# A 3200-point filter by FFT, then a gated convolution: the transform factored as 100 by 32 instead of 128 by 25

## The chip, the cores and the metric

The kernel runs on one core of a Trainium2 chip. The core has a matrix engine (TensorE, PE in the profile; PEld is its loading of weights), a vector engine (VectorE, DVE), an activation engine (ScalarE, ACT), a general one (GpSimd, POOL) and SyncE (SP), which here only issues transfers; 16 DMA engines move the data. Each engine works through its own queue in order and waits on semaphores. Matmuls write to PSUM, and ACT or DVE must copy ("evict") the result to SBUF. The metric is device time in microseconds. The kernel before took 382.9 us (median of three runs, 381.12 to 385.6).

## What is computed

For each of 8 sequences of 3200 positions by 256 channels, a global filter in the frequency domain, and then a gated linear unit whose gate is a causal convolution of 5 taps.

```python
X = np.fft.rfft(x, axis=1)                       # x: 8 x 3200 x 256
x = np.fft.irfft(X * (filt_r + 1j*filt_i), n=3200, axis=1)
gate_pre = sum(conv_w[k] * xp[:, k:k+S, :] for k in range(5))   # xp: x with 4 zero rows ahead
out = (1/(1+np.exp(-gate_pre)) * (x @ w_val)) @ w_out
```

Inputs and output are float32.

## The kernel before, in words

The transform of 3200 is split as 128 by 25 (`L`, `R`). Everything is done per sequence ("batch") in chunks, and the tables of sines and cosines are made on the core in a set-up part (lines 91 to 284, mostly DVE, with ACT's Sin and POOL's iota).

- `load_x` (L86): POOL issues a transfer that also casts to bf16; seven chunks of 3 or 4 residues (`PCH`), 128 partitions each.
- `s1` (L307): a matmul with `cf_t` does the 128-point transform; DVE evicts to `so` (L310), SP writes it to a DRAM scratch `dscr` (L312).
- `load_t` (L326 to L329): after all seven chunks, SP reads `dscr` back in another order, so that the 25 residues of 5 frequencies lie on 125 partitions (`tt`). This trip through DRAM is the forward relayout.
- `s2` (L340 to L346): twiddle and 25-point transform as one real matrix per group of 5 frequencies; 13 groups, two to a chunk, four matmuls of 125x128 weights by 256 columns each. ACT evicts to `xs` (L349). DVE multiplies by the filter (`za` L354, `zb` L358) and adds (`z` L360).
- `inva` (L376, L378): the inverse of that, again four matmuls of 256 columns per group; ACT evicts to `u` (L381), SP writes a second scratch `escr` (L392).
- `load_v`, `invb` (L413): `escr` is read back as `vt`; one matmul of 128 columns per residue and channel half; ACT evicts to `yt` (L415) with the channels on the partitions. POOL copies a small halo (L420, L422).
- `conv` (L431): the five taps as 64x64 diagonal matmuls, 20 to a chunk; ACT evicts with Sigmoid to `gt` (L436). `val` (L448): four matmuls; DVE multiplies by the gate (`gv`, L453). `outp` (L465): two matmuls per residue; DVE or ACT by turns evict to `o` (L470, L473), SP stores it (L475).

All stages share one PSUM pool of four buffers of 128 x 1024 float32. The order of the work is a hand-written loop: at each step, a chunk of every stage, each with a fixed lag (`LAG_S2`, `LAG_IB`), so that several batches are under way at once; each evicting engine is fixed by the stage.

Of the kernel before, what the change touches and what calls it, by code (L numbers as in the profile page):

```python
# [15 lines left out]
PI = math.pi  # L16

L = 128
R = 25
NG = 13
GL = 5
NQ = 2 * NG
P2 = GL * R

PCH = [(0, 4), (4, 4), (8, 4), (12, 3), (15, 3), (18, 3), (21, 4)]
ICH = [PCH[-1]] + PCH[:-1]  # L30
GCH = [(0, 2), (2, 2), (4, 2), (6, 2), (8, 2), (10, 2), (12, 1)]
NCH = 7
# [3 lines left out]
def kernel(  # L36
# [9 lines left out]
):  # L46
    nc = tc.nc
    B, S, D = x.shape
    N = S
    K = moe_conv_w.shape[0]  # L50
    assert D == 256 and S == L * R and K == 5
    H = K - 1

    cpool = ctx.enter_context(tc.tile_pool(name="const", bufs=1))
    cf_t = cpool.tile([128, 130], FP16, name="cf_t")
    ci_t = cpool.tile([128, 128], FP16, name="ci_t")
    wc_t = cpool.tile([128, NG, 128], FP16, name="wc_t")
    ws_t = cpool.tile([128, NG, 128], FP16, name="ws_t")
    wsn_t = cpool.tile([128, NG, 128], FP16, name="wsn_t")
    vc_t = cpool.tile([128, NG, 128], FP16, name="vc_t")  # L60
    vs_t = cpool.tile([128, NG, 128], FP16, name="vs_t")
    vsn_t = cpool.tile([128, NG, 128], FP16, name="vsn_t")
    fr_t = cpool.tile([128, NG, D], BF16, name="fr_t")
    fm_t = cpool.tile([128, NG, 2, D], BF16, name="fm_t")
# [3 lines left out]
    b_npi = cpool.tile([128, 1], FP32, name="b_npi")  # L68
# [3 lines left out]
    xpool = ctx.enter_context(tc.tile_pool(name="xin", bufs=10))  # L72
    spool = ctx.enter_context(tc.tile_pool(name="s1o", bufs=4))
    tpool = ctx.enter_context(tc.tile_pool(name="s2i", bufs=8))
# [4 lines left out]

    xts = {}  # L80

    def load_x(b, j):
        p0, np_ = PCH[j]
        xt = xpool.tile([128, 4, D], BF16, name="xt")
        src = x[b].rearrange("(a r) d -> a r d", r=R)[:, p0:p0 + np_, :]
        nc.gpsimd.dma_start(out=xt[:, 0:np_, :], in_=src)  # L86
        xts[(b, j)] = xt

    for j in range(NCH):
        load_x(0, j)  # L90


    with tc.tile_pool(name="gen", bufs=1) as g1, \
         tc.tile_pool(name="gen2", bufs=2) as g2, \
         tc.tile_pool(name="genf", bufs=1) as gf:

        def floormod(src_ap, divisor):
            shp = list(src_ap.shape)
            divi = g2.tile(shp, I32, name=f"fm_i{shp[1]}")
            bak = g2.tile(shp, FP32, name=f"fm_b{shp[1]}")  # L100
            q = g2.tile(shp, FP32, name=f"fm_q{shp[1]}")
            cm = g2.tile(shp, FP32, name=f"fm_c{shp[1]}")
            nc.vector.tensor_scalar(divi[...], src_ap, 1.0 / float(divisor), None,
                                    op0=ALU.mult)
            nc.vector.tensor_copy(bak[...], divi[...])
            nc.vector.scalar_tensor_tensor(q[...], bak[...], -float(divisor), src_ap,
                                           op0=ALU.mult, op1=ALU.add)
            nc.vector.tensor_scalar(cm[...], q[...], float(divisor) - 0.5, None,
                                    op0=ALU.is_ge)
            nc.vector.scalar_tensor_tensor(q[...], cm[...], -float(divisor), q[...],  # L110
                                           op0=ALU.mult, op1=ALU.add)
            nc.vector.tensor_scalar(cm[...], q[...], -0.5, None, op0=ALU.is_lt)
            nc.vector.scalar_tensor_tensor(q[...], cm[...], float(divisor), q[...],
                                           op0=ALU.mult, op1=ALU.add)
            return q

        def iota(shape, pattern, base, cm, name):
            t = g1.tile(shape, FP32, name=name)
            nc.gpsimd.iota(t[...], pattern=pattern, base=base, channel_multiplier=cm,
                           allow_small_or_imprecise_dtypes=True)  # L120
            return t

        nc.vector.memset(b_npi[:, :], -PI)
        pcol = iota([128, 1], [[0, 1]], 0, 1, "pcol")


        kc = iota([128, NG, 2, GL], [[5, NG], [0, 2], [1, GL]], 1, 0, "kc")
        nc.vector.memset(kc[:, NG - 1, 0, GL - 1:GL], 0.0)
        pr = g1.tile([128, NG, 2, GL], FP32, name="pr")
        nc.vector.tensor_scalar(pr[...], kc[...], pcol[:, 0:1], None, op0=ALU.mult)  # L130
        nc.vector.tensor_scalar(pr[:, :, 0, :], pr[:, :, 0, :], 0.75 * L, None,
                                op0=ALU.add)
        q = floormod(pr[...].rearrange("p g c l -> p (g c l)"), L)
        nc.scalar.activation(cf_t[:, :], q[...], AF.Sin, bias=b_npi[:, 0:1],
                             scale=2.0 * PI / L)

        ident = g1.tile([128, 128], FP32, name="ident")
        nc.vector.memset(ident[:, :], 1.0)
# [3 lines left out]
        idh = g1.tile([128, 128], FP16, name="idh")  # L142
        nc.vector.tensor_copy(idh[:, :], ident[:, :])


        rq = floormod(pcol[...], R)
        lp = g1.tile([128, 1], FP32, name="lp")
        nc.vector.tensor_tensor(lp[...], pcol[...], rq[...], op=ALU.subtract)
        nc.vector.tensor_scalar(lp[...], lp[...], 1.0 / R, None, op0=ALU.mult)
        rp = g1.tile([128, 1], FP32, name="rp")  # L150
        nc.vector.tensor_copy(rp[...], rq[...])
        lw = g1.tile([128, 1], FP32, name="lw")
        nc.vector.tensor_scalar(lw[...], pcol[...], 4.0 * R - 0.5, None, op0=ALU.is_ge)
        nc.vector.tensor_scalar(lw[...], lw[...], -65.0, None, op0=ALU.mult)


        mk = g1.tile([128, GL, R], FP16, name="mk")
        mkf = g1.tile([128, GL, R], FP32, name="mkf")
        nc.vector.memset(mkf[...], 1.0)
        nc.gpsimd.affine_select(out=mkf[...], in_=mkf[...], pattern=[[-R, GL], [0, R]],  # L160
                                compare_op=ALU.is_ge, fill=0.0, base=0,
                                channel_multiplier=1)
        nc.gpsimd.affine_select(out=mkf[...], in_=mkf[...], pattern=[[R, GL], [0, R]],
                                compare_op=ALU.is_ge, fill=0.0, base=R - 1,
                                channel_multiplier=-1)
        nc.vector.tensor_copy(mk[...], mkf[...])

        def expand(dst, src):
            nc.gpsimd.memset(dst[:, :, P2:128], 0.0)
            for g in range(NG):  # L170
                nc.vector.tensor_tensor(
                    dst[:, g, 0:P2].rearrange("p (l r) -> p l r", l=GL),
                    src[:, g, :].unsqueeze(1).to_broadcast((128, GL, R)),
                    mk[...], op=ALU.mult)

        def negate(dst, src):
            nc.vector.tensor_scalar(dst[...], src[...], -1.0, None, op0=ALU.mult)

        def sincos(prod, dc, ds, dsn):
            qs = floormod(prod[...].rearrange("p g r -> p (g r)"), N)  # L180
            sn = g2.tile([128, NG, R], FP16, name="sn")
            nc.scalar.activation(sn[...].rearrange("p g r -> p (g r)"), qs[...],
                                 AF.Sin, bias=b_npi[:, 0:1], scale=2.0 * PI / N)
            pc = g2.tile([128, NG, R], FP32, name="pc")
            nc.vector.tensor_scalar(pc[...], prod[...], 0.75 * N, None, op0=ALU.add)
            qc = floormod(pc[...].rearrange("p g r -> p (g r)"), N)
            cs = g2.tile([128, NG, R], FP16, name="cs")
            nc.scalar.activation(cs[...].rearrange("p g r -> p (g r)"), qc[...],
                                 AF.Sin, bias=b_npi[:, 0:1], scale=2.0 * PI / N)
            expand(dc, cs)  # L190
            expand(dsn, sn)
            negate(ds, dsn)

        HK = R // 2 + 1
        kv = g1.tile([128, NG, R], FP32, name="kv")
        nc.gpsimd.iota(kv[:, :, 0:HK], pattern=[[5, NG], [L, HK]], base=1,
                       channel_multiplier=0, allow_small_or_imprecise_dtypes=True)
        nc.gpsimd.iota(kv[:, :, HK:R], pattern=[[5, NG], [-L, R - HK]],
                       base=1 + L * (R - 1), channel_multiplier=0,
# [352 lines left out]
```

## Time and profile before

| what | value |
|---|---|
| runs | 385.6, 381.12, 382.9 us; median 382.9 |
| profiled execution: its span, first to last instruction | 385.9 us (0.8% above the median of the runs) |
| granted clock, mean over the span | 0.966 |
| PE, DVE, ACT, POOL busy | 312.3, 284.9, 229.1, 64.2 us |
| DMA | 94.53 MB, mean 245 GB/s |
| first eviction of stage 2 (`xs`), first of the inverse (`yt`) | 47.1 us, 93.7 us |
| first `out` matmul of each batch | 116.1, 154.4, 193.2, 233.7, 273.6, 310.0, 342.6, 364.6 us |

The page gives no other time for the profiled execution than its span. The page counts an engine as busy from an instruction's start to its end. Matmuls are pipelined, so neighbours overlap and a PE that is always "busy" need not be streaming all the time. "Slices" are 40 equal parts of the span (9.65 us each), with the busy share in tenths. "Stretches" give for a window the busy time and number of instructions of each engine, then the granted clock, the DMA share and GB/s. The timeline lists start, duration, engine, line, operation, output from input, tile shape and count, and in brackets the idle time ahead and what ended it.

### The profile page before, as it was taken

What the parts mean: (1) busy time and instruction counts of PE and PEld (TensorE: products, weight loads), DVE (VectorE), ACT (ScalarE), POOL (GpSimd) and SP (SyncE); (2) the same over time, 40 slices, a digit from 0 to 9 for tenths busy, and PEclk for the clock granted to TensorE, in tenths of its full rate; (3) what the DMA queues carried; (4) which work ended last, traced back from release to release, by engine and by line L of the source; (5) the groups of instructions that cost most, each with busy time, mean ns of one, the idle gap of its engine ahead of it and who ended that gap; (6) DMA issues with size and microseconds to landing.
All of it is one profiled execution on the core that took longest, in us unless ns stands there. A gap on an engine that the chain in (4) does not pass through costs nothing.

```text
span 385.9 us, 8019 instructions
## 1 busy us (share of the span) xinstructions
PE 312.3 (81%) x3089; PEld 206.9 (54%) x3089; DVE 284.9 (74%) x462; ACT 229.1 (59%) x255; POOL 64.2 (17%) x131
## 2 busy tenths in 40 slices
PE   0230477475899999999997999899999999999992
PEld 0100145253656756766675666566676677666661
DVE  4999958553858887888787789678977677765554
ACT  1100235334976777677765776677677878867660
POOL 8797211112110211021102011100010001001000
PEclk9999998766989999999999999999999999999998
DMA  7999999999999999999999999989595968449343
GB/s 124 144 162 190 216 257 251 231 250 280 179 250 249 311 286 273 263 282 332 274 301 303 286 269 298 285 299 319 201 351 170 304 223 299 136 142 323 141 191 152
DMA packets 94118, 94.53 MB, mean 245 GB/s; under 512 B 10102, under 2 KB 74624, under 8 KB 94080
## 3 DMA queue, kind: packets, MB, share of 16 engines
q1 hardware_dynamic: 80064, 78.98, 62.5%
q0 software_dynamic: 14016, 15.04, 28.1%
q8 instruction: 24, 0.39, 0.4%
q14 instruction: 14, 0.11, 0.1%
HBM read 56.59 MB, written 52.43 MB: 282 GB/s over the span
## 4 chain that ended last, share of the span: by engine, by line
PE 44%; DVE 20%; DMA 19%; SPq 8%; issue 4%; ACT 2%; POOL 1%; DVEq 0%; ACTq 0%; POOLq 0%
PE ps L431 12%; PE ps L448 7%; DMA escr<-u 6%; PE ps L465 6%; DVE so L310 6%; DMA vt<-escr 5%; SPq L326 5%; PE ps L413 5%; DMA dscr<-so 4%; PE ps L376 3%; DVE gv L453 3%; DMA tt<-dscr 3%; PE ps L378 3%; PE ps L307 3%; DVE za L354 2%
## 5 line engine op out<-in xcount | busy, mean ns | idle before, releaser
L415 ACT ACTIVATE yt<-ps 128x1024 bf16<-128x1024 f32 (+1 forms) x56 | 52.1, 931 | 44.3 <-PE ps L413 44.2
L453 DVE TENSOR_TENSOR gv<-ps,gt 128x1024 bf16<-128x1024 f32 (+1 forms) x56 | 61.9, 1104 | 18.7 <-PE ps L448 13.7
L310 DVE CAST so<-ps 128x1024 bf16<-128x1024 f32 (+1 forms) x56 | 61.5, 1103 | 19.0 <-PE ps L307 15.9
L354 DVE TENSOR_TENSOR za<-xs,fr_t 125x1024 bf16<-125x1024 bf16 (+1 forms) x56 | 37.3, 665 | 50.5 <-ACT xs L349 50.3
L381 ACT ACTIVATE u<-ps 125x1024 bf16<-125x1024 f32 (+1 forms) x56 | 53.9, 963 | 24.4 <-PE ps L378 21.6
L431 PE MATMUL ps<-yt,dg_t 64*64 64x512 bf16 (+1 forms) x1120 | 65.7, 361 | 0.8
L349 ACT ACTIVATE xs<-ps 125x1024 bf16<-125x1024 f32 (+1 forms) x56 | 54.0, 965 | 19.6 <-PE ps L346 18.4
L436 ACT ACTIVATE gt<-ps 128x1024 bf16<-128x1024 f32 (+1 forms) x56 | 52.4, 935 | 9.1 <-PE ps L431 5.9
L86 POOL DMA_DIRECT2D xt<-in_x_dram x56 | 30.2, 569 | 153.0 <-PE ps L307 146.5
L307 PE MATMUL ps<-xt,cf_t 128*128 128x512 bf16 x112 | 36.9, 421 | 22.4 <-DVE so L310 11.4
L465 PE MATMUL ps<-wo_t,gv 128*128 128x256 bf16 x400 | 52.8, 273 | 0.9 <-DVE gv L453 0.9
L448 PE MATMUL ps<-yt,wv_t 128*128 128x512 bf16 (+1 forms) x224 | 52.6, 357 | 0.0
L465 PEld LDWEIGHTS <-gv 128*128 128x128 bf16 x400 | 39.1, 98 | 14.9 <-DVE gv L453 1.2
L413 PE MATMUL ps<-ci_t,vt 128*128 128x128 f16 x400 | 31.9, 221 | 13.3 <-DMA vt<-escr 9.6
L431 PEld LDWEIGHTS <-dg_t 64*64 64x64 bf16 x1120 | 30.1, 106 | 23.2 <-issue 10.1
L340 PE MATMUL ps<-tt,wc_t 125*128 125x256 bf16 x104 | 30.1, 289 | 12.9 <-DMA tt<-dscr 10.6
L470 DVE COPY o<-ps 128x1024 f32<-128x1024 f32 (+1 forms) x32 | 36.7, 1148 | 1.1 <-PE ps L465 1.1
L360 DVE TENSOR_TENSOR z<-za,zb 125x1024 bf16<-125x1024 bf16 (+1 forms) x56 | 36.4, 650 | 1.3
L413 PEld LDWEIGHTS <-vt 128*128 128x128 bf16 x400 | 27.0, 98 | 17.9 <-DMA vt<-escr 10.7
L358 DVE TENSOR_TENSOR zb<-xs,fm_t 125x1024 bf16<-125x1024 bf16 (+1 forms) x56 | 36.2, 646 | 0.0
L376 PE MATMUL ps<-z,vc_t 125*128 125x256 bf16 x104 | 30.0, 289 | 6.9 <-DVE z L360 6.9
L307 PEld LDWEIGHTS <-cf_t 128*128 128x128 f16 x112 | 9.2, 108 | 41.7 <-issue 28.2
(109 smaller groups left out, 386.6 us busy)
## 6 DMA issues: line engine op xcount, KB each, us to landing
out_dram<-o SPq DMA_DIRECT2D x32, 512.0 KB
tt<-dscr SPq DMA_DIRECT2D x48, 256.0 KB
escr<-u SPq DMA_DIRECT2D x48, 224.0 KB
out_dram<-o SPq DMA_DIRECT2D x24, 384.0 KB
xt<-in_x_dram POOLq DMA_DIRECT2D x32, 256.0 KB, 6.5
dscr<-so SPq DMA_DIRECT2D x32, 256.0 KB
vt<-escr SPq DMA_DIRECT2D x32, 256.0 KB
xt<-in_x_dram POOLq DMA_DIRECT2D x24, 192.0 KB, 5.7
```

The costliest lines, as they stand in the source:

```text
L307: nc.tensor.matmul(ps[:, a * D:e * D], lhsT=cf_t[:, 0:128], rhs=xt[:, a:e, :], start=True, stop=True)
L310: nc.vector.tensor_copy(so[:, 0:np_, :].rearrange("p a d -> p (a d)"), ps[:, 0:np_ * D])
L349: nc.scalar.activation(xs[0:P2, 0:ng, :, :].rearrange("p g c d -> p (g c d)"), ps[0:P2, 0:ng * 512], AF.Copy)
L354: nc.vector.tensor_tensor(za[0:P2, 0:ng], xs[0:P2, 0:ng], fr_t[0:P2, g0:g0 + ng, :].unsqueeze(2).to_broadcast((P2, ng, 2, D)), op=ALU.mult)
L381: nc.scalar.activation(u[0:P2, 0:2 * ng, :].rearrange("p q d -> p (q d)"), ps[0:P2, 0:ng * 512], AF.Copy)
L413: nc.tensor.matmul(ps[:, o:o + L], lhsT=v[:, a, 128 * dh:128 * dh + 128], rhs=ci_t[:, :], start=True, stop=True)
L415: nc.scalar.activation(y[:, :, H + p0:H + p0 + np_, :].rearrange("p h a n -> p h (a n)"), ps[:, :].rearrange("p (h n) -> p h n", h=2)[:, : ...
L431: nc.tensor.matmul(ps[64 * dh:64 * dh + 64, 512 * r:512 * r + np_ * L], lhsT=dg_t[rows, dh, k, :], rhs=y[rows, dh, p0 + k:p0 + k + np_, :] ...
L436: nc.scalar.activation(g[:, :, 0:np_ * L], ps[:, :].rearrange("p (h n) -> p h n", h=2)[:, :, 0:np_ * L], AF.Sigmoid)
L448: nc.tensor.matmul(ps[:, 512 * eh:512 * eh + np_ * L], lhsT=wv_t[:, dh, 128 * eh:128 * eh + 128], rhs=y[:, dh, H + p0:H + p0 + np_, :], st ...
L453: nc.vector.tensor_tensor(gv[:, :, 0:np_ * L], ps[:, :].rearrange("p (h n) -> p h n", h=2)[:, :, 0:np_ * L], g[:, :, 0:np_ * L], op=ALU.mult)
L465: nc.tensor.matmul(ps[:, D * a:D * a + D], lhsT=gv[:, eh, L * a:L * a + L], rhs=wo_t[:, eh, :], start=(eh == 0), stop=(eh == 1))
```

## The change

The transform is factored as 100 by 32. The real input makes 51 of the 100 first-stage frequencies enough, kept as two halves of 26 with real and imaginary part, each padded to 32 rows: four quarters of 32 partitions.

- Stage 1 takes the 256 channels as 128 pairs, and for all 32 residues of a batch evicts into one tile `so` (pair, residue, two channels; runs of 4 residues x 2 channels). It has one buffer.
- The forward relayout is four DVE instructions per batch (`turn`): transposes of 32x32 blocks of 4-byte words (a word is a pair of bf16), from `so` to `tt`, within each quarter. The scratch `dscr` and both its transfers are gone.
- Stage 2 is a 64x64 matmul per frequency of 256 columns, read from `tt` as pairs 128 bytes apart; real and imaginary parts are the two halves of the 64. Four such matmuls stand on the four quadrants of the array. Its inverse `inva` is two of them per frequency, on `za` (spectrum times filter's real part) and `zb` (times its imaginary part); they are summed in PSUM, so that the DVE addition `z` is gone.
- The inverse relayout still goes through the scratch `escr`, now in single writes of 128 partitions; its reads are split into 96 and 8 partitions, the output stores into 96 and 4. The x loads have 100 partitions and eight chunks.
- The order is no longer the loop with lags. A list scheduler (`Plan`) is given every task with an engine, a cost in us, a rank (its place in time, eight ranks to a batch), what it depends on and the buffers it takes and gives; it plays the tasks through and writes the queues of all engines in that order. Evictions `so`, `xs`, `u`, `o` go to ACT or DVE, whichever the plan finds free (as planned, ACT has 159 full and 8 half ones, DVE 65 and 8). The plan charges 0.1 us for a change between 64x64 and whole-array matmuls, and prefers to stay.
- The tables are made in fewer, larger DVE operations (`frac` in place of `floormod`), with three 128 x 1664 products on POOL.

```diff
-L = 128
-R = 25
+L = 100
+R = 32
...
     def s1(b, j):
+        xt = st.pop(("X", b, j))
+        xv = xt[0:L].rearrange("p r (q e) -> p q r e", e=2)
         ps = psum()
+        for h in range(2):
+            nc.tensor.matmul(ps[:, 512 * h:512 * h + 512],
+                             lhsT=cf_t[0:L].rearrange("p h c i -> p (h c i)"),
+                             rhs=xv[:, 64 * h:64 * h + 64], start=True, stop=True)
...
+    def so(b, j, e):
+        if ("SO", b) not in st:
+            st["SO", b] = sopool.tile([128, DP, R, 2], BF16, name="so")
+        ps = st.pop(("s1", b, j))
+        copy(e, st["SO", b][:, :, RC * j:RC * j + RC, :].rearrange("p q r e -> p q (r e)"),
+             ps[:, :].rearrange("p (q n) -> p q n", q=DP))
...
+        dst = st["T", b][:, w * q:w * q + w].rearrange("p q r e -> p (q r e)").bitcast(FP32)
+        nc.vector.transpose(dst, src)
...
     def s2(b, u):
+        for a in range(nm):
+            for h, t in ((0, 0), (1, 1), (0, 1), (1, 0)):
+                i = 2 * (m0 + a) + t
+                rows = slice(64 * h, 64 * h + 64)
+                nc.tensor.matmul(ps[64 * t:64 * t + 64, 512 * h + D * a:512 * h + D * a + D],
+                                 lhsT=w_t[rows, i, :], rhs=t_[rows, :, i, :],
+                                 start=True, stop=True)
...
     def inva(b, u):
+            for w, tab in enumerate((a_t, b_t)):
+                for t, h in ((0, 0), (1, 1), (0, 1), (1, 0)):
+                    rows = slice(64 * t, 64 * t + 64)
+                    nc.tensor.matmul(
+                        ps[64 * h:64 * h + 64, 512 * t + D * a:512 * t + D * a + D],
+                        lhsT=tab[rows, NM * h + m0 + a, :],
+                        rhs=zz[w][rows, h, D * a:D * a + D],
+                        start=(w == 0), stop=(w == 1))
...
+        nc.sync.dma_start(out=v[0:96], in_=sv[0:96])
+        nc.sync.dma_start(out=v[96:NV], in_=sv[96:NV])
...
+        nc.sync.dma_start(out=dst[0:96], in_=o[0:96])
+        nc.sync.dma_start(out=dst[96:L], in_=o[96:L])
...
+    plan = Plan(dict(ps=4, xt=NXT, so=1, t=2, xs=3, za=3, zb=3, u=4, e=2, v=NVB, y=2, g=NGB,
+                     gv=NGB, o=NOB))
...
+            add(f"s1{b},{j}", {"PE": 0.45}, t0 + j, dep, lambda e, b=b, j=j: s1(b, j),
+                take=("ps",) + (("so",) if j == 0 else ()), give=("xt",), mode=0)
+            add(f"so{b},{j}", two(0.97, 1.15), t0 + j, [f"s1{b},{j}"],
+                lambda e, b=b, j=j: so(b, j, e), give=("ps",))
...
+            add(f"t{b},{q}", {"DVE": 1.15}, t0 + NCH, [f"so{b},{j}" for j in range(NCH)]
+                + ([f"t{b},{q - 1}"] if q else []),
+                lambda e, b=b, q=q: turn(b, q), take=("t",) if q == 0 else (),
+                give=("so",) if q == 3 else ())
...
+            add(f"wr{b},{u}", {"SP": 0.45}, r + 1, [f"ue{b},{u}"] + ([f"wr{b},{u - 1}"] if u else []),
+                lambda e, b=b, u=u: wr(b, u), take=("e",) if u == 0 else (), land=3.0)
...
+            add(f"lv{b},{i}", {"SP": 0.8}, r - 2, [f"wd{b},{u}" for u in range(len(UCH))],
+                lambda e, b=b, i=i: lv(b, i), take=("v",), land=3.0,
+                give=())
```

More of the change, by code (lines that the diff above doesn't have):

```diff
@@ L16, with __init__, add, run @@
 PI = math.pi
-L = 128
-R = 25
[L24 to L32, printed above, removed]
+L = 100
+R = 32
+NS = 26
+NM = 13
+NV = 4 * NS
+RC = 4
+NCH = R // RC
+UCH = [(m, min(2, NM - m)) for m in range(0, NM, 2)]
+ICH = [NCH - 1] + list(range(NCH - 1))
+MAGIC = 12582912.0
+class Plan:
+    def __init__(self, room, stay=1.0):
+        self.tasks, self.room, self.stay = {}, dict(room), stay
+    def add(self, name, engines, rank, deps, emit, take=(), give=(), land=0.0, mode=None):
+        self.tasks[name] = dict(engines=engines, rank=rank, deps=deps, emit=emit, take=take,
+                                give=give, land=land, mode=mode)
+    def run(self):
+        left = dict(self.tasks)
+        users, need = {}, {}
+        for n, t in left.items():
+            need[n] = len(t["deps"])
+            for d in t["deps"]:
+                users.setdefault(d, []).append(n)
+        ready_at = {n: 0.0 for n in left}
+        free = {}
+        mode = None
+        gives = []
+        ready = {n for n in left if need[n] == 0}
+        order = []
+        now = 0.0
+        while left:
+            gives.sort()
+            while gives and gives[0][0] <= now + 1e-9:
+                for pool in gives.pop(0)[1]:
+                    self.room[pool] += 1
+            best = None
+            for n in ready:
+                t = left[n]
+                if ready_at[n] > now + 1e-9:
+                    continue
+                if any(self.room[p] < 1 for p in t["take"]):
+                    continue
+                for e, cost in t["engines"].items():
+                    if free.get(e, 0.0) <= now + 1e-9:
+                        away = e == "PE" and t["mode"] != mode
+                        key = (t["rank"] + (self.stay if away else 0.0), cost)
+                        if best is None or key < best[0]:
+                            best = (key, n, e, cost)
+            if best is None:
+                later = [ready_at[n] for n in ready if ready_at[n] > now + 1e-9]
+                later += [v for v in free.values() if v > now + 1e-9]
+                later += [g[0] for g in gives if g[0] > now + 1e-9]
+                assert later, ("stuck", sorted(ready)[:20], self.room)
+                now = min(later)
+                continue
+            _, n, e, cost = best
+            t = left.pop(n)
+            ready.discard(n)
+            for p in t["take"]:
+                self.room[p] -= 1
+            if e == "PE":
+                if t["mode"] != mode:
+                    cost += 0.1
+                mode = t["mode"]
+            end = now + cost
+            free[e] = end
+            if t["give"]:
+                gives.append((end + 0.1, t["give"]))
+            for u in users.get(n, ()):
+                need[u] -= 1
+                ready_at[u] = max(ready_at[u], end + 0.1 + t["land"])
+                if need[u] == 0:
+                    ready.add(u)
+            order.append((t["emit"], e))
+        self.span = max(free.values())
+        return order
@@ L52 @@
     H = K - 1
+    DP = D // 2
     cpool = ctx.enter_context(tc.tile_pool(name="const", bufs=1))
[L55 to L64, printed above, removed]
+    cf_t = cpool.tile([128, 2, 2, 32], FP16, name="cf_t")
+    ci_t = cpool.tile([128, L], FP16, name="ci_t")
+    w_t = cpool.tile([128, NS, 64], FP16, name="w_t")
+    a_t = cpool.tile([128, NS, 64], FP16, name="a_t")
+    b_t = cpool.tile([128, NS, 64], FP16, name="b_t")
+    fr_t = cpool.tile([128, 2, NM, D], BF16, name="fr_t")
+    fi_t = cpool.tile([128, 2, NM, D], BF16, name="fi_t")
     dg_t = cpool.tile([128, 2, K, 64], BF16, name="dg_t")
@@ L89 @@
[L89 to L135, printed above, removed]
@@ L152 @@
[L152 to L162, printed above, removed]
@@ L163 @@
[L163 to L174, printed above, removed]
@@ L255 @@
-        sincos(nv, vc_t, vs_t, vsn_t)
-        ac = g1.tile([128, 1], FP32, name="ac")
-        nc.vector.memset(ac[...], 2.0)
-        for i in (123, 124):
-            nc.gpsimd.affine_select(out=ac[...], in_=ac[...], pattern=[[0, 1]],
-                                    compare_op=ALU.not_equal, fill=1.0, base=-i,
-                                    channel_multiplier=1)
-        ps = psum()
-        nc.tensor.matmul(ps[:, 0:128], lhsT=cf_t[:, 0:128], rhs=idh[:, :],
-                         start=True, stop=True)
@@ L525 @@
+    add("setup", {"none": 0.0}, -100, [], None, land=22.0)
+    add("pool", {"none": 0.0}, -100, [], None, land=18.0)
+    plan.room["xt"] -= NCH
+    order = plan.run()
+    with tc.manual_schedule(engines={mybir.EngineType.PE, mybir.EngineType.DVE,
+                                     mybir.EngineType.Activation, mybir.EngineType.SP,
+                                     mybir.EngineType.Pool}):
+        for emit, e in order:
+            if emit is not None:
+                emit(e)
 _INS = ['x', 'filt_r', 'filt_i', 'moe_w_val', 'moe_conv_w', 'moe_w_out']
```

613 lines of the change are left out of this document (334 added, 279 removed).

## The prediction

> **What bounds the kernel now.** I read the page's busy shares and slices first, then its queues, then busy time and DMA share by stretch, then the timeline, which gives each operation's price.
>
> ```profile
> PE 312.3 (81%) x3089; PEld 206.9 (54%) x3089; DVE 284.9 (74%) x462; ACT 229.1 (59%) x255; POOL 64.2 (17%) x131
> ...
> PE   0230477475899999999997999899999999999992
> ...
> DMA  7999999999999999999999999989595968449343
> ...
> q1 hardware_dynamic: 80064, 78.98, 62.5%
> q0 software_dynamic: 14016, 15.04, 28.1%
> ...
> 120.00:280.00 160.00, 150.82 (x1566) 103.14 (x1564) 128.67 (x161) 114.18 (x126) 16.86 (x34) 1.00 0.98 284
> 300.00:360.00 60.00, 60.00 (x691) 40.70 (x692) 40.06 (x49) 46.63 (x55) 2.59 (x6) 1.00 0.71 232
> ```
>
> The DMA engines are busy over 90% in nearly every slice to slice 28; in 120-280 us their share is 0.98 while PE is busy 94%, DVE 80%, ACT 71%. Once the x loads are over (300-360) DMA falls to 0.71 and PE is busy throughout. So the middle is set by DMA and PE together, the end by PE. The first stage-2 eviction (xs) starts at 47.1 us and the first inverse eviction (yt) at 93.7: a quarter of the span is set-up and filling.
>
> ```profile
> 200.03 0.28 PE L340 MATMUL ps<-tt,wc_t 125*128 125x256 bf16 x1
> 200.14 0.27 PE L342 MATMUL ps<-tt,ws_t 125*128 125x256 bf16 x1
> ...
> 201.00 1.01 PE L431 MATMUL ps<-yt,dg_t 64*64 64x384 bf16 x20
> 201.94 0.50 PE L307 MATMUL ps<-xt,cf_t 128*128 128x512 bf16 x2
> ...
> 172.52 1.02 ACT L415 ACTIVATE yt<-ps 128x1024 bf16<-128x1024 f32 x1
> 173.43 1.03 ACT L349 ACTIVATE xs<-ps 125x1024 bf16<-125x1024 f32 x1
> ...
> 180.33 0.69 DVE L354 TENSOR_TENSOR za<-xs,fr_t 125x1024 bf16<-125x1024 bf16 x1 [0.96 <-ACT xs L349]
> 180.94 0.68 DVE L358 TENSOR_TENSOR zb<-xs,fm_t 125x1024 bf16<-125x1024 bf16 x1
> ...
> 182.27 1.22 DVE L310 CAST so<-ps 128x1024 bf16<-128x1024 f32 x1
> 183.40 1.22 DVE L453 TENSOR_TENSOR gv<-ps,gt 128x1024 bf16<-128x1024 f32 x1
> ```
>
> Prices are start to start, since neighbours overlap by about 0.1 us. A matmul of 256 columns takes 0.109 us; the single records give 0.056 for 128, 0.162 for 384, 0.216 for 512, so 100 take 0.044 and 400 take 0.169. The 20 conv matmuls of 64x64 run four abreast: 0.94 us for 7680 columns. Their records start 4 ns apart in fours, one four every 0.162 us, and each change between 64x64 and whole-array work costs 0.093 us. ACT takes 0.91 us for 1024 PSUM columns (0.70 for 768, so 0.73 for 800); DVE 1.13 from PSUM (0.90 for 800) and 0.60 for a bf16 product of 1024.
>
> **PE.** Per batch, before: s1 2.7, stage 2 and inverse-a 52 matmuls of 0.109 each (5.7 + 5.7), inverse-b 2.8, conv 6.75, val 5.4, out 5.45, together 34.5; with 14 mode changes, 35.8. After: s1 16 x 0.216 = 3.45; stage 2 13 fours x 0.109 = 1.42; inverse-a 26 fours = 2.84; inverse-b 64 x 0.044 = 2.8; conv 40 fours x 0.169 = 6.77; val 32 x 0.169 = 5.4; out 64 x 0.109 = 7.0: 29.7. The instruction order has 142 mode changes in all, 13.2 us. Sum 8 x 29.7 + 13 = 251 us against 286. The new first and last stages pad 25 residues to 32 and lose 2.3 us a batch; the tiles win 7.1.
> Unknown: s1 and stage 2 now stream pairs of elements from strided places, and the inverse fours take 256 columns where conv's take 384 or more. Rows bound it by 0.109 a four (contiguous) and 0.109 for each of its members (none abreast). I take 0.109 a four, since L431 has the same row, column and bank order. [...] No strided stream is in this trace.
>
> **DVE and ACT.** Counted in the order of instructions. ACT: 128 yt and gt x 0.73, 159 evictions x 0.91, 8 halves x 0.5 = 242 us. DVE: 64 gv x 0.90 = 58; 112 products 63 (the 56 sums z are gone, added up by PE); 32 transposes; 65 evictions x 1.13 = 73, 8 halves 5. A transpose has no row: 1024 four-byte elements lie between the bf16 product's 0.60 and two passes at 2.26; I take 1.13, the one-per-cycle row it is nearest to, so 36. Sum 235 us. The so evictions write runs of 16 bytes; no row has that either, between 0.91/1.13 and double; I take the former, since rows of other layouts do not differ. Per batch that is 30.3 and 29.4 us beside PE's 31.3: three engines at one level.
>
> **DMA and queues.** The dscr write and tt read are gone. From the mean times of single packets: x 800 of 0.225 us, escr writes 3328 of 0.029, vt 832 of 0.094, out 800 of 0.163, over 16 engines 11.2 + 6.0 + 4.9 + 8.2 = 30.3 us a batch; before, the same way, 40.4, which is the period of the middle (38.3 to 40.5). SP issues 39 transfers a batch instead of 44, and the stalls of L326's issues (SPq, 8% of the chain) go. A landing of escr then vt takes about 9 us in the chain (4.5 to 6.3, then 3.5 to 5.0) against 3 + 3 in the planner; ib has some three chunks (12 us) between its data's rank and its own, so I cost it nothing in the middle. If that cover is gone it is 3 us a batch, 24 in all.
> New waits: stage 2 waits for four transposes, they for all eight so; with one so buffer the next batch's s1 stands behind them in PE's queue. In the middle conv, val and out are queued ahead of it; at the start it shows, 4.5 us.
>
> **Start and sum.** POOL issues 8 x loads, 8 filter and 8 small loads (0.57 to 0.78 each), 11 iotas and three 1664-column products (2 to 3.2 each, by the copy's 1.2 and the iota's 1.9 ns a column); the last table is with DVE at about 25 us, and DVE's set-up ends near 31. Then 4 so, 4 transposes: first xs at 41 (47.1 before). Ahead of the first yt the order puts nearly all of batch 1's front: 37 us of DVE work, first yt near 73 (93.7 before).
> Left for PE then: eight back halves of 22.0 (176), six fronts of 7.7 less one s1 (43), 12 of changes: 231 us. Before, PE streamed or switched 92% of the DMA-bound middle and 98% of 300-360. DMA at 30.3 of about 32 is near, not at, its limit; I take 95%: 243. From the last matmul to the end it was 5.8. Sum 73 + 243 + 6 = 322 us of span against 385.9. The profiled span is 0.8% above the median of the runs, 382.9; in the runs' measure 320.
>
> **Rivals.**
> B, strided streams at half rate: s1 and stage 2 cost 4.9 us more a batch, 26 after 73 us: 75 + 257/0.95 + 6 = 351. For it: the pairs. Against: nothing in the trace.
> C, transposes at 2.26 us: the first yt comes 11 us later, the rest hides under PE: 333.
> [...]
> E, slower: a fixed order over engines at one level makes PE wait at the PSUM hand-off. There are four buffers and about 390 uses after 73 us; my 95% allows 0.03 us each. It decides at (386 - 79 - 231)/390 = 0.2 us a use; at 0.25 the span is 73 + 231 + 97 + 6 = 407. For it: evictions fill 30 of 32 us, and a tile's own hold (stream, 0.27 tail and hand-off, eviction; 97 us a batch over four buffers) already takes 24. Against: hand-offs in the trace are 0.04 (PE to ACT) and 0.05 us (back), and PE stood at 98% with ACT at 78%.
> F, the new tiles do not run abreast: 39 fours cost 3 x 0.109 more, 12.8 us a batch, 77 after 73 us: 73 + 308/0.95 + 6 = 403. Against: L431.
>
> **Chances.** Forecast 0.60 (own range 304 to 338: PE at 100% to 90%, start 5 us either way), B 0.12, C 0.08, D 0.07, E 0.09, F 0.04. Range 302 to 356 takes in B, C and D. A measurement of this kernel tells apart about 1%. Faster 0.86 (the forecast and B to D, less a little), same 0.02, slower 0.12 (E and F, without those just under the bound).
>
> **What would show it.** Stage 2's records in fours 0.109 us apart (B: 0.2; F: single); transposes 1.1 us each (C); first yt near 73; DMA share near 0.9 in the middle with x landing in about 6 us (D: 10 or more); PE's busy share over 90% after 80 us, and no eviction engine named as what PE waits for over 0.1 us a tile (E). It is wrong if the middle's period is over 36 us a batch; then the row that PE waits for names the rival.

## The result, and the profile after

The changed kernel took 380.68 us (median of 20 runs, 376.25 to 386.75), against 384.10 for the kernel before in runs beside it (median of 20, 380.28 to 389.49). Some executions of either kernel are 1 to 3% slower than its fastest, and the ratios here and below are those of the fast ones alone: 0.989, with an interval of 0.985 to 0.992. It is faster by about 1%, that is, nearly the same, where 16% was forecast (320 us, range 302 to 356). The profiled execution has a span of 375.8 us, 1.3% below the median of the runs, where that of before lay 0.8% above. So the two spans differ by more than the kernels do, and the working below is in spans.

The page of the kernel after: busy time of the engines; then, in 40 slices, PE's busy share, the granted clock and the DMA share; then the two queues.

```profile
PE 308.6 (82%) x3936; PEld 190.5 (51%) x3936; DVE 279.3 (74%) x365; ACT 267.5 (71%) x302; POOL 71.3 (19%) x128
...
PE   0340158496999999899999999899999999999993
...
PEclk9985558877899999899999999999999999999998
DMA  7999979479679986989779986985485548868644
...
q1 hardware_dynamic: 44896, 55.20, 49.7%
q0 software_dynamic: 13056, 15.08, 31.2%
```

PE's slices stand at 8 and 9 from the eleventh to the last but one; before, they did so too, but for one 7. DMA has room now. The 3936 matmuls keep PE as busy (308.6 us) as the 3089 before (312.3), though 35 us of streaming should have gone.

Busy time by stretch (us; PE, PEld, DVE, ACT and POOL with counts; then clock, DMA share, GB/s), same kernel:

```profile
100.00:140.00 40.00, 40.00 (x522) 26.04 (x522) 28.85 (x33) 32.37 (x38) 5.57 (x11) 1.00 0.83 209
180.00:220.00 40.00, 39.08 (x508) 24.96 (x507) 32.31 (x38) 33.95 (x40) 5.54 (x11) 1.00 0.86 214
```

PE is busy 98 to 100% in these two, DVE 72 to 81%, ACT 81 to 85%, and DMA is down from 0.98 to about 0.85. In the stretches between and behind them (140 to 180 and 220 to 260 us) PE is busy 94%. What PE waits for in 120 to 280 us is little: 4.0 us for `vt` and 2.1 for `gv`. So the middle is set mainly by PE. The first inverse evictions (yt) of the eight batches are at 93.2, 118.5, 157.9, 197.6, 237.3, 275.6, 312.7 and 342.2 us. The period there is 37 to 40 us, much as before (38 to 41), and not the 31 to 33 of the forecast. PE is nearly full, so either it has more to do than counted, or what it does takes longer. The groups by line and shape (busy us, mean ns of one, then idle time ahead and what ended it) say which:

```profile
L369 PE MATMUL ps<-xt,cf_t 100*128 100x512 bf16 x128 | 64.5, 609 | 36.2 <-DVE so L362 18.7 <-DMA fr_t<-in_filt_r_dram 15.9 <-ACT so L360 1.4
L387 DVE STREAM_TRANSPOSE tt<-so 128x1024 f32<-128x1024 f32 x32 | 38.7, 1227 | 2.7 <-ACT so L360 2.6
L397 PE MATMUL ps<-tt,w_t 64*64 64x256 bf16 x416 | 36.0, 412 | 12.9 <-DVE tt L387 10.1 <-DVE gv L524 2.6 <-ACT u L360 0.2
L428 PE MATMUL ps<-za,a_t 64*64 64x256 bf16 x416 | 29.4, 287 | 0.7 <-ACT xs L360 0.7
```

L397 and L428 issue the same 416 matmuls in the same fours; only the place they read from differs. L428 reads 256 neighbouring elements, L397 pairs that lie 128 bytes apart: 412 ns against 287. From start to start at full clock, L428's fours stand 0.109 us apart and L397's 0.20 to 0.23, 0.21 in the mean. Stage 1 (L369), whose pairs lie 512 bytes apart, has a mean of 609 ns for 512 columns and stands 0.42 us apart instead of 0.216; two lines of the timeline show it:

```profile
52.12 1.04 PE L369 MATMUL ps<-xt,cf_t 100*128 100x512 bf16 x2
116.53 1.04 PE L369 MATMUL ps<-xt,cf_t 100*128 100x512 bf16 x2
```

Before, two such matmuls took 0.50 us together. These are the two strided streams, at half rate. Priced so, PE streams 274 us and changes mode for 13, 287 in all; before it was 286.

The first stage-2 eviction (xs) is at 52.2 us, where 41 was forecast. In the timeline of the set-up (start, duration, engine, line, operation; in brackets the idle time ahead and what ended it) three things are late:

```profile
18.85 1.10 DVE L208 TENSOR_SCALAR gg<-gg 128x1664 f32<-128x1664 f32 x1 [7.32 <-POOL gg L272]
20.45 7.93 DVE L345 TENSOR_SCALAR dg_t<-ident,cw 64x64 bf16<-64x64 f32 x1 [0.44 <-POOL ident L327]
20.95 3.73 POOL L250 TENSOR_TENSOR tba<-gg,ea 128x1664 f32<-128x1664 f32 x1
24.62 3.70 POOL L250 TENSOR_TENSOR tbb<-gg,eb 128x1664 f32<-128x1664 f32 x1
```

DVE waits 7.3 us for POOL's first product. Then a DVE operation that takes about 0.25 us elsewhere (255 ns, the mean of 20 in the kernel before) lasts 7.93 us, to 28.38, when the second of POOL's two other products has just ended (28.32). The first stage-1 matmul also starts only at 15.9 us, behind the clearing of `cf_t`, which stands on POOL behind the issues of the filter's loads.

### The profile page after: what moved, and what is told of

Its sections match the earlier page's. It is cut to its first block, busy times and chain, and to the rows that moved or that the text cites. A ratio compares the mean times of both kernels' runs of the same rounds, so it can differ in the third digit from the quotient of the medians.

```text
span 375.8 us, 9658 instructions
## 1 busy us (share of the span) xinstructions
PE 308.6 (82%) x3936; PEld 190.5 (51%) x3936; DVE 279.3 (74%) x365; ACT 267.5 (71%) x302; POOL 71.3 (19%) x128
## 4 chain that ended last, share of the span: by engine, by line
PE 55%; DVE 21%; DMA 9%; ACT 5%; issue 4%; POOL 3%; SPq 1%; POOLq 0%; ACTq 0%; DVEq 0%
PE ps L534 13%; PE ps L496 11%; PE ps L369 9%; PE ps L514 7%; DMA vt<-escr 7%; DVE tt L387 7%; PE ps L397 6%; PE ps L469 5%; PE ps L428 4%; DVE gv L524 4%; DVE dg_t L345 3%; DMA xt<-in_x_dram 2%; ACT so L360 2%; DVE so L362 1%; ACT o L360 1%
## 5 line engine op out<-in xcount | busy, mean ns | idle before, releaser
L369 PE MATMUL ps<-xt,cf_t 100*128 100x512 bf16 x128 | 64.5, 609 | 36.2 <-DVE so L362 18.7
L524 DVE TENSOR_TENSOR gv<-ps,gt 128x800 bf16<-128x800 f32 x64 | 62.7, 981 | 23.1 <-PE ps L514 14.8
L360 ACT ACTIVATE so<-ps 128x1024 bf16<-128x1024 f32 x50 | 51.1, 1024 | 40.1 <-PE ps L369 25.8
L360 ACT ACTIVATE o<-ps 100x1024 f32<-100x1024 f32 x59 | 60.7, 1028 | 18.5 <-PE ps L534 14.2
L534 PE MATMUL ps<-wo_t,gv 128*100 128x256 bf16 x512 | 69.0, 278 | 1.5 <-DVE gv L524 1.0
L496 PE MATMUL ps<-yt,dg_t 64*64 64x400 bf16 x1280 | 66.6, 337 | 0.0
L534 PEld LDWEIGHTS <-gv 128*100 128x100 bf16 x512 | 54.3, 126 | 21.6 <-issue 12.7
L505 ACT ACTIVATE gt<-ps 128x800 bf16<-128x800 f32 x64 | 53.6, 839 | 4.6 <-PE ps L496 3.7
L479 ACT ACTIVATE yt<-ps 128x800 bf16<-128x800 f32 x64 | 53.2, 837 | 4.7 <-PE ps L469 4.6
L514 PE MATMUL ps<-yt,wv_t 128*128 128x400 bf16 x256 | 53.9, 333 | 0.0
L397 PE MATMUL ps<-tt,w_t 64*64 64x256 bf16 x416 | 36.0, 412 | 12.9 <-DVE tt L387 10.1
L387 DVE STREAM_TRANSPOSE tt<-so 128x1024 f32<-128x1024 f32 x32 | 38.7, 1227 | 2.7 <-ACT so L360 2.6
L369 PEld LDWEIGHTS <-cf_t 100*128 100x128 f16 x128 | 12.0, 104 | 56.0 <-DMA xt<-in_x_dram 19.6
L428 PE MATMUL ps<-zb,b_t 64*64 64x256 bf16 x416 | 28.2, 279 | 4.4 <-DVE zb L415 4.4
```

Source lines behind the costliest of these rows:

```text
L360: nc.scalar.activation(dst, src, AF.Copy, **kw)
L369: nc.tensor.matmul(ps[:, 512 * h:512 * h + 512], lhsT=cf_t[0:L].rearrange("p h c i -> p (h c i)"), rhs=xv[:, 64 * h:64 * h + 64], start=Tr ...
L387: nc.vector.transpose(dst, src)
L397: nc.tensor.matmul(ps[64 * t:64 * t + 64, 512 * h + D * a:512 * h + D * a + D], lhsT=w_t[rows, i, :], rhs=t_[rows, :, i, :], start=True, s ...
L496: nc.tensor.matmul(ps[64 * dh:64 * dh + 64, 512 * r:512 * r + RC * L], lhsT=dg_t[rows, dh, k, :], rhs=y[rows, dh, RC * j + k:RC * j + k + ...
L505: nc.scalar.activation(g[...], ps[:, :].rearrange("p (h n) -> p h n", h=2)[:, :, 0:RC * L], AF.Sigmoid)
```

## The experiments

Two theories stood at the start. **Stride**: stage 1 and stage 2 stream at half rate because each run of neighbouring elements is short, and with the runs made longer the time falls. **Hand-off** (rival E): PE is busy because the records overlap, but the fixed order over engines near one level is what sets the period; making streams faster then moves the waits and not the time. Beside them, the start and the landing of `vt` were open. The kernel before was run beside each group again: 385.95 us with e1 to e4, 383.19 with e5 to e8, 386.18 with e9 to e12. Across groups the ratios to it are the fairer measure.

**e1, stage 1 reads whole rows.** The pairing of channels is left to the eviction, which then reads PSUM in pairs 1 KB apart.

```diff
...
-  rhs=xv[:, 64 * h:64 * h + 64]
+  rhs=xt[0:L, 2 * h:2 * h + 2, :]
...
-  ps[:, :].rearrange("p (q n) -> p q n", q=DP)
+  ps[:, :].rearrange("p (r q e) -> p q r e", r=RC, e=2)
```

> Stage 1 streams its 512 columns as they lie in the x tile (contiguous), and the eviction does the pairing instead, reading PSUM in pairs 1 KB apart; the result is the reference's. Theory S (strided streams make PE the bound again): the stage-1 matmuls go from 0.42 to 0.22 us apart, PE needs 128 x 0.21 = 27 us less, of which some 20 us lie after the filling, and the time falls by 12 to 24 us against the changed kernel (to about 357 to 368), unless the eviction now pays for the stride: then ACT's and DVE's so rise above 1.02 and 1.22 us and eat the gain. Theory E (the fixed order and the PSUM hand-off hold PE): the matmuls get faster but PE waits longer, and the time stays within 4 us of 380.

368.44 us (368.23 to 370.34), ratio to before 0.956 [0.952, 0.960]. The groups of stage 1 and its evictions:

```profile
L360 ACT ACTIVATE so<-ps 128x1024 bf16<-128x1024 f32 x50 | 51.1, 1025 | 23.3 <-PE ps L368 9.8 <-DVE tt L386 8.9 <-ACT gt L504 3.6
L368 PE MATMUL ps<-xt,cf_t 100*128 100x512 bf16 x128 | 42.7, 436 | 36.9 <-DVE so L362 19.7 <-POOL cf_t L228 15.4 <-ACT so L360 1.8
```

The matmul stands 0.22 us apart again, and the eviction, which now carries the stride, takes 1025 ns as in the changed kernel (1024). So the stride costs PE, not ACT. But the matmul stands so only where the granted clock is full. Two lines of this run, at a granted clock of 0.5 (0.58 in the mean of 40 to 60 us) and of 1.0 (100 to 140 us):

```profile
51.55 1.03 PE L368 MATMUL ps<-xt,cf_t 100*128 100x512 bf16 x2
115.21 0.60 PE L368 MATMUL ps<-xt,cf_t 100*128 100x512 bf16 x2
```

At 0.5 the contiguous stream stands 0.38 to 0.43 us apart, and the strided one of the changed kernel 0.42 to 0.44 (its line at 52.12 us above; granted clock 0.50 in 51 to 54 us): there the stride costs next to nothing. Of the 128 matmuls 22 lie in such stretches here, and the 9 at the very start, where the views print a clock of 1.00, nevertheless stand 0.40 to 0.43 apart. So PE saved about 97 x 0.20 = 20 us, and 12 reach the time: between 140 and 260 us PE now streams 80% and changes mode 4%. The chain of waits of this kernel (start, us, what) shows the same place in each batch:

```profile
182.62 1.03 ACT o L360
184.87 7.04 DMA vt<-escr
192.05 0.51 PE ps L468 x8
...
222.10 1.03 ACT o L360
224.34 6.53 DMA vt<-escr
231.00 0.82 PE ps L468 x8
```

and the timeline of SyncE's queue shows what `vt` was behind:

```profile
183.67 0.32 SPq L547 DMA_DIRECT2D out_dram<-o  x1
184.03 0.33 SPq L548 DMA_DIRECT2D out_dram<-o  x1
184.46 0.32 SPq L458 DMA_DIRECT2D vt<-escr  x1
```

The read of `vt` needs no `o`, but it stands in SP's queue behind the store that waits for the eviction of `o` at 182.62; then it needs 7 us to land, and the planner had charged 3. PE stands waiting for it, 8.3 us in 120 to 280. This is the cover that the prediction costed at nothing.

**e2, stage 2 reads whole rows**, and the transposes write each 4-byte word 512 bytes from the last.

```diff
-  tpool.tile([128, DP, 32, 2], BF16, name="tt")
+  tpool.tile([128, 32, DP, 2], BF16, name="tt")
...
-  rhs=t_[rows, :, i, :]
+  rhs=t_[rows, i, :, :]
```

> The transposes write tt frequency by frequency, so that stage 2 streams 256 contiguous columns; the transpose now writes its 4-byte words 512 bytes apart. Theory S: a four of stage 2 goes from 0.20 to 0.11 us, 104 x 0.09 = 9 us of PE, 6 to 9 us less in time, if the transpose stays at 1.23 us; if it pays for the stride (2.3 us), 32 x 1.1 = 34 us of DVE come on and the time rises by 10 us or more. Theory E: within 4 us of the changed kernel.

390.19 us (10 runs, 384.91 to 399.62), ratio 1.001 [0.996, 1.005], where the changed kernel has 0.989: slower than it by about 1%.

```profile
L387 DVE STREAM_TRANSPOSE tt<-so 128x1024 f32<-128x1024 f32 x32 | 60.5, 1920 | 2.6 <-ACT so L360 2.6
...
L397 PE MATMUL ps<-tt,w_t 64*64 64x256 bf16 x416 | 23.0, 291 | 22.1 <-DVE tt L387 14.3 <-DVE gv L524 7.6 <-ACT u L360 0.2
```

Stage 2's fours are at 0.109 us now, as the stride theory says, but the transpose rose from 1227 to 1920 ns. The stride went from PE to DVE, where 22 us was paid for about 10 (104 fours x 0.10), and PE's wait for `tt` rose from 10.1 to 14.3 us.

**e3, two table products on DVE instead of POOL.**

```diff
-  table(a_t, ..., "a", nc.gpsimd);  table(b_t, ..., "b", nc.gpsimd)
+  table(a_t, ..., "a", V);          table(b_t, ..., "b", V)
```

> Only the two 128 x 1664 sums of the set-up move from GpSimd to DVE. Theory P (GpSimd's tensor operations hold a DVE instruction up: the one at 20.45 us lasts until both are over): DVE's 7.9 us instruction falls to 0.3, two of 1.9 come on, the set-up on DVE ends 4 to 9 us before 42.2, and the time falls by as much. Rival (DVE waited for the tables anyway): the end of the set-up stays within 2 us.

377.63 us (374.55 to 380.67), ratio 0.976 [0.968, 0.983], 3 us below the changed kernel, 5 by the ratios. The timeline of its set-up:

```profile
20.41 0.25 DVE L345 TENSOR_SCALAR dg_t<-ident,cw 64x64 bf16<-64x64 f32 x1 [0.44 <-POOL ident L327]
20.57 1.88 DVE L250 TENSOR_TENSOR tba<-gg,ea 128x1664 f32<-128x1664 f32 x1
```

The operation that lasted 7.93 us takes 0.25, and the product that took POOL 3.73 takes DVE 1.88. DVE's set-up ends at 38.3 instead of 42.2 us, and the first yt is at 89.2 instead of 93.2. In the profiled execution (379.88 us) these 4 us are lost again behind the first yt, so the gain in time rests on the other three runs and on e5.

**e4 and e8, how long must a run be?** Stage 1 streams runs of 8 and of 4 elements (16 and 8 bytes), still 512 bytes apart; the pairing of the channels is left out, and only the time is read.

```diff
-  xv = xt[0:L].rearrange("p r (q e) -> p q r e", e=2)
+  xv = xt[0:L].rearrange("p r (q e) -> p q r e", e=8)
...
-  rhs=xv[:, 64 * h:64 * h + 64]
+  rhs=xv[:, 16 * h:16 * h + 16]
```

In e8 it is `e=4` and 32 in place of 16.

> Stage 1 streams runs of 8 elements (16 bytes) in place of 2, with the same step between runs of one position; which channels are paired is then wrong, and only the time of the stage-1 matmuls is looked at. [...] If any jump costs, they stay above 0.25 us.

> As the run with runs of 8, but with runs of 4 elements (8 bytes): channels are paired wrongly, and only the stage-1 matmuls are looked at. [...]

369.97 and 369.60 us (one run each; e1 has 368.44). From start to start at full clock, the matmul of 512 columns takes 0.42 us with runs of 2, 0.223 to 0.228 with runs of 4, and mostly 0.220 with runs of 8 or with whole rows. So with pairs each new place takes about 1.6 ns (0.42 us over 256 places), which is close to what four neighbouring elements take (0.216 us over 128). In stage 1 runs of four are all but free; runs of two cost double. Pairs nearer than 128 bytes were not tried.

**e5, e1 and e3 together.**

> The two edits together: stage 1 contiguous (alone 368.4 us) and the set-up sums on DVE (alone 377.6). If both work on parts of the time that follow each other (the start and the middle), the gains add up: 12 + 3 us off 380.7, 365 us. If the filling behind the start hides one, 368.

363.12 us (362.43 to 365.16), ratio 0.948 [0.943, 0.952]. The two gains add up: it is 5 us below e1 (3 by the ratios), and its first yt is at 87.4 us against 92.1 there.

**e6, the planner told the true landings** (on e5).

```diff
-  lambda e, b=b, u=u: wr(b, u), ..., land=3.0)
+  lambda e, b=b, u=u: wr(b, u), ..., land=5.0)
...
-  lambda e, b=b, i=i: lv(b, i), ..., land=3.0,
+  lambda e, b=b, i=i: lv(b, i), ..., land=6.5,
```

> As the last, but the scheduler is told that escr's writes land after 5.0 us and vt's loads after 6.5 instead of 3.0 each (what the traces show, 4.5 to 6.3 and 6.5 to 7.0); nothing else is changed, and only the order of the queues differs. With stage 1 contiguous PE streams only 75 to 80% of the middle, and once a batch the chain goes through an eviction of o, its store, the vt load behind it on SP and a landing of 7 us. Theory L (the wait for vt, which the plan has too short): PE fills the wait with other work, some 3 to 5 us a batch, and the time falls by 10 to 25 us. Rival (the middle is set by the PSUM hand-off and the eviction engines): within 4 us of the last.

376.57 us (375.19 to 378.30), ratio 0.982 [0.977, 0.986]: 13 us slower than e5, where a gain was expected. PE's wait for `vt` all but went (0.3 us between 120 and 280 us; 8.3 in e1), but the list came out in another order. The first yt is at 97.9 instead of 87.4 us, and PE waits for other rows instead (`gv` 1.9 us, `zb` 1.7, `u` 1.2). Most of the loss (10.5 us) is the start; why the scheduler puts more ahead of the first yt was not followed further.

**e7, output stores issued by GpSimd** (on e5), so that `vt` has no store ahead of it on SP.

```diff
-  nc.sync.dma_start(out=dst[0:96], in_=o[0:96])
+  nc.gpsimd.dma_start(out=dst[0:96], in_=o[0:96])
...
-  add(f"st{b},{j}", {"SP": 0.8}, ...
+  add(f"st{b},{j}", {"POOL": 1.2}, ...
```

> As e5, but the output stores are issued by GpSimd, so that the vt loads do not stand behind a store that waits for its eviction on SP. Theory Q (the place in SP's queue is what makes vt late): the vt wait of 6 to 7 us a batch shrinks by 1 to 3 us and the time falls by 8 to 20 us. Theory L: the landing itself is the wait; the time stays within 4 us, or rises if GpSimd's x loads are late behind the stores.

360.49 us (358.95 to 361.62), ratio 0.939 [0.935, 0.943]. The period is an even 35.0 us, and in 120 to 280 us PE no longer waits for `vt` at all (7.6 us in e5). From the first yt to the last matmul it is 261 us against 268 in e5. Part of this gain is given back at the end, where the last stores are issued by GpSimd: from the last matmul to the end it is 10 us, where the changed kernel has 6.

**e9, stage 2's stream alone** (on e7). It reads whole rows from the old layout, which leaves out the choice of the frequency; the transposes stay as they are.

```diff
-  rhs=t_[rows, :, i, :]
+  rhs=t_[rows, 4 * i:4 * i + 4, :, :]
```

> As e7, but stage 2 streams 256 elements as they lie (contiguous, of the wrong frequencies), the transposes untouched: only the price of its pair stream is taken away. A four goes from 0.20 to 0.11 us, 9.5 us of PE in all. If PE is what bounds e7's middle (period 35.0 us, PE streaming or switching 88%), the time falls by 4 to 8 us from 360.5; if the hand-off does, by less than 2.

347.04 us (345.81 to 348.55), ratio 0.900 [0.891, 0.908]: 13 us below e7, 15 by the ratios. That is too much for some 10 us of streaming, and the surplus is probably a side effect. Each matmul now reads what one transpose wrote and need not wait for all four, so its first xs and yt come earlier (xs 46.7 instead of 48.8, yt 84.5 instead of 89.0). From the first yt matmul to the last `out` matmul it is 251 us against 261: 10 us are the stream's, as e10 bears out, which has no such side effect.

**e10, runs of 4 for stage 2 as well** (on e7): the transposes put the words of two pairs side by side, 8 bytes, so that a run is again four elements.

```diff
-  tpool.tile([128, DP, 32, 2], BF16, name="tt")
+  tpool.tile([128, DP // 2, 32, 4], BF16, name="tt")
...
-  dst = ....bitcast(FP32)
+  dst = ....bitcast(FP32).rearrange("p (q r w) -> p q w r", r=32, w=2)
```

> As e7, but the transposes write the words of two channel pairs side by side, so that stage 2 streams runs of 4 elements (8 bytes); the result is the reference's. By e8 a run of 4 streams at 0.44 ns a column, so a four takes 0.11 us. The transpose now writes its words 8 bytes apart: if only far steps cost it (512 bytes: 1.92 us), it stays at 1.23 us and the time falls as in e9; if every step that is not one word costs, it goes to 1.9 and the time rises by 5 to 10 us.

351.62 us (350.98 to 352.39), ratio 0.911 [0.904, 0.918], 9 us below e7, 11 by the ratios.

```profile
L387 DVE STREAM_TRANSPOSE tt<-so 128x1024 f32<-128x1024 f32 x32 | 39.8, 1260 | 0.7 <-ACT so L360 0.7
...
L397 PE MATMUL ps<-tt,w_t 64*64 64x256 bf16 x416 | 25.9, 317 | 11.8 <-DVE tt L387 7.7 <-DVE gv L524 3.2 <-ACT u L360 0.6
```

Writing words 8 bytes apart costs the transpose 33 ns, not 700, and the fours stand 0.13 to 0.14 us apart instead of 0.20 to 0.23: nearer to the 0.109 of neighbouring elements, but not at it. The yt-to-last-matmul stretch is 252 us, as in e9.

**e11, the rest of the start** (on e7): the first product and the clearing of `cf_t` on DVE too.

```diff
-  nc.gpsimd.tensor_tensor(gg ...)    nc.gpsimd.memset(cf_t ...)
+  V.tensor_tensor(gg ...)            V.memset(cf_t ...)
```

> As e7, with the last tensor work of the set-up taken off GpSimd: the product gg and the four clears of cf_t go to DVE, so that stage 1 doesn't wait behind the filter loads on GpSimd's queue (first matmul 16.4 us) and DVE doesn't wait 7.8 us for gg. First xs moves from 48.8 to 41 to 44 us and the time falls by 4 to 8 us. Rival (the filter or x transfers set the start): less than 2 us.

355.35 us (352.95 to 357.42), ratio 0.920 [0.911, 0.930], 5 us below e7, 7 by the ratios. The first xs is at 41.9 us, where the prediction had it, but by another path: the `so` evictions and the transposes are now done in the middle of the set-up, and what PE waits for ahead of the first stage 2 is an x load of the next batch, which lands at 40.2 us. The first yt is at 82, still not 73.

**e12, e10 and e11 together.**

> e10 and e11 together: if the start and the middle add up, 346 to 352 us.

346.44 us (345.12 to 349.83), ratio 0.899 [0.890, 0.908]: the best version, faster than both kernels. Its page's busy line and one stretch:

```profile
PE 283.1 (81%) x3936; PEld 188.6 (54%) x3936; DVE 275.4 (79%) x372; ACT 264.2 (76%) x302; POOL 126.4 (36%) x249
```

```profile
180.00:220.00 40.00, 38.84 (x585) 27.98 (x584) 36.22 (x42) 36.88 (x44) 16.28 (x32) 1.00 0.92 246
```

The period is 34 us. PE, DVE, ACT and DMA stand at 97, 91, 92 and 92% of the stretch, against 98, 81, 85 and 86% in the changed kernel: now the middle is as level as the prediction saw it. PE streams or changes mode 93% of it.

## Why the prediction was wrong, point by point

In spans, 322 us was forecast and 375.8 came: 20 us of the 54 lie ahead of the first yt (73 against 93.2), 34 between it and the last matmul (243 against 277), and none in the tail (6 and 6.0).

- **The step that failed most: "I take 0.109 a four" for stage 2, and 0.216 for stage 1.** The prediction said that no strided stream was in the trace, kept both bounds, and took the fast end, because L431 had the same rows, columns and banks. But L431 streams neighbouring elements, so it was no row for this. The measured prices are 0.42 us and 0.21 us (0.20 to 0.23): against the sum 26 us more for stage 1 and about 10 for stage 2, which is all of the 35 us that PE was to save. Some three quarters of it lie after the first yt, where rival B had 26. Shown by e1 (12 us of time; the other 8 of its 20 are not seen in the time, with `vt` holding PE back), e9 and e10 (10 us between first yt and last matmul), e4 and e8 (with the same steps, only longer runs, the rate is back). Rival B, with a chance of 0.12, was the right mechanism; in spans it came to 351 and not 376, since it had nearly the same early start (18 us of the 25) and 6 us less behind it.
- **"DVE's set-up ends near 31", "first xs at 41", "first yt near 73": three sizes too small.** The set-up ended at 42.2, xs was at 52.2, yt at 93.2. The prediction had counted POOL's products at 2 to 3.2 us each, but as work of POOL alone. They took 2.99 to 3.73, DVE waited 7.3 us for the first, and the other two held a DVE operation for 7.93 us (e3: 0.25 when they are gone). Moving all of it to DVE gives the first xs at 41.9 (e11), though DVE then has more to do. By what mechanism the products held that operation is not shown: its record starts 0.5 us ahead of the first product (20.45 and 20.95 us) and ends with the second (28.38 and 28.32), and why it got no turn between the two is left open. The other 9 us lie between xs and yt: 40 us in e11 and 41 in the changed kernel, 32 forecast. In e12 the chain there has one wait of 7.8 us, ACT's evictions `u` behind the write of `escr`; it was not tried apart. Nor was the clock: every price of the forecast was taken at full clock, and the granted clock in the changed kernel is 0.59 in 40 to 60 us, 0.78 in 60 to 80 and 0.83 in 80 to 100 (before, 0.74 in 60 to 100). So the cause of these 9 us stays open.
- **The landing of `vt`, costed "nothing in the middle": wrong once PE is fast.** In the changed kernel PE waits for `vt` 4.0 us in 120 to 280 us; with stage 1 fast it is 8.3 us (e1), and the time gains only 12 of 20. The prediction's price if the cover was gone, 24 us, was too high: taking the stores out of its way (e7) gave 7 us between first yt and last matmul, of which 2.6 reach the time, with 4 lost again at the end. The reason it gave for the cover, three chunks between rank and use, overlooked SP's queue, where `vt` waits behind stores that wait for evictions.
- **Right:** the inverse's fours at 0.109 us (F refuted), inverse-b 0.044, conv and val 0.169, `out` 0.109 and changes 0.093 us. Transposes take 1.23 us by the record, 1.16 from start to start, for the 1.13 of the row of 1024 PSUM columns (C refuted); what DVE does in a cycle, no run shows. Evictions are unchanged by their 16-byte runs (`so` 1024 ns by ACT and 1220 by DVE; before, 1024 columns took 1024 and 1218). The DMA share is 0.83 to 0.86 in 100 to 220 us (0.9 forecast), and the x loads of 100 rows land in 6.1 us and not in 10 or more (D), so D did not set the time. Rival D of the chances, that x loads of 100 rows lie on fewer than the 16 DMA engines, was a guess of the author's: on how many engines they lie, no view shows. The line of the x loads follows (issue, count, KB, us to landing).

```profile
xt<-in_x_dram POOLq DMA_DIRECT2D x64, 200.0 KB, 6.1
```

- **E, the hand-off, did not decide.** In the changed kernel PE streams or changes mode about 92% of the middle (120 to 280 us), and each faster stream that was not paid for elsewhere (as in e2) shortened the time. The 95% assumed for the middle is near what e12 shows (93%) once the streams have their price. Its remaining distance to the forecast (348.1 of span against 322) is 10 us of start, 4 of tail from GpSimd's stores, and 12 between, where stage 2 stands at 0.13 to 0.14 and not 0.109, and PE streams or changes mode only about 62% of the 18 us after the first yt matmul, at prices of full clock, while the granted clock is 0.72 in 83 to 100 us.
- The sentence "it is wrong if the middle's period is over 36 us a batch; then the row that PE waits for names the rival" was half right: the period was 37 to 40 us, but PE waited for little, and for nothing that named the rival. It showed in the spacing of PE's own records, which the paragraph also named (B: 0.2).
- A reading to set right, on which no term of the sum rests: of the chain before, SPq has 8% in all and L326's issues 5%.

## What to carry to other kernels

When a change reorders data so that a matmul streams it from strided places, price that stream by a row with the same length of run and at the same granted clock; a row with the same shape but neighbouring elements says nothing about it (here 0.216 us for 512 columns, where the pairs took 0.42). In a copy between, look for the cheapest place to pay for the stride: here PSUM reads by ACT and DVE in pairs were free (1025 and 1216 ns against 1024 and 1220), transposes that write 8-byte runs nearly so (1260 ns against 1227), and matmul streams of 4-byte runs twice as dear at full clock (0.42 us for 512 columns against 0.22). And when the bounding engine gets faster, look at once for a transfer that stands in its issuing queue behind one that waits for something else.

## What the runs showed of the hardware that was not expected

- A matmul's moving stream of bf16 pairs takes about 1.6 ns for each pair: 512 columns take 0.42 us in runs of 2, 0.223 to 0.228 in runs of 4, mostly 0.220 in runs of 8 and above. Pairs 128 and 512 bytes apart are alike (0.21 us over 128 places in stage 2, four matmuls abreast, and 0.42 over 256).
- This price did not follow the granted clock: at 0.5 the pairs take 0.42 to 0.44 us for 512 columns, as at 1.0, while the contiguous stream takes 0.38 to 0.43 there (e1) and 0.22 at 1.0. At half clock the stride was nearly free.
- Evictions by ACT and DVE that read PSUM in pairs 1 KB apart take the same time as contiguous ones (1025 and 1216 ns, e1; 1024 and 1220 in the changed kernel).
- A 32x32 transpose of 4-byte words, 128 x 1024, takes 1227 ns; with its output words 8 bytes apart 1260, and 512 bytes apart 1920.
- Two products of 128 x 1664 float32 on GpSimd (3.7 us each) held a small DVE operation for 7.93 us; on DVE such a product takes 1.88.
- Giving the list scheduler truer landing times made the kernel 13 us slower (e6): the wait that it removes (8.3 us in e1, 0.3 in e6) did not show this.
